# Element-wise work of a fused attention, gate and mixer kernel moved from VectorE to GpSimd and ScalarE

## The chip, the cores and the metric

The kernel runs on one core of a Trainium2 chip. The metric is the device time of one execution in microseconds (us), the median of several runs. Five engines work side by side and each takes its instructions in order: TensorE (PE in the rows, PEld for its weight loads), VectorE (DVE), ScalarE (ACT), GpSimd (POOL) and SyncE (SP), which here issues the DMA transfers.

## What is computed

Three blocks follow one another, all in float32. Shapes: 4 batches, 8 heads, 576 tokens, head width 64, model width 512, a causal convolution of 5 taps.

```python
scores = q @ k.T / sqrt(D)                    # keep the 32 largest of each row
attn = softmax(where(scores >= kth, scores, -1e9)); x = attn @ v

gate = sigmoid(sum_k conv_w[k] * x_shifted[k])          # 5 taps
x = (gate * (x @ w_val)) @ w_out

theta = x @ w_theta
y = w_tok_r @ (x * cos(theta)) + w_tok_i @ (x * sin(theta))
u = x + y
out = u + relu(u @ w_ch)
```

## The kernel before

**Attention.** The heads are taken in 16 pairs (units), four to a batch, and each unit in 9 tiles of 128 rows by 576 columns of scores: 144 tiles. One step of the main loop (lines 1269 to 1271) handles one tile. VectorE carries most of a step: `pick` (L524, L528, L530) finds the 24 largest of each row in pieces, `below` and `rest` (L537, L550) the last 8, `select` (L559 to L564) the threshold for three tiles at once, `mask` (L611) applies it. ScalarE empties the scores (L499), counts (L545) and makes the exponentials (L174); TensorE makes scores (L485, L486), transposes (L624, L628) and the product with v (L704). When a unit is closed (`close`), its normalised result goes to a buffer `xT` (L722), of which there are 5, and the convolution's five taps are summed to the gate: tap 0 and those in `CT` by ScalarE (L747, L750), each of the latter added by GpSimd (L751), the rest by VectorE (L759).

**The later blocks.** The work of gate and mixer is written as generators in a list `jobs`: `front(b)` makes the products `pval` (x @ w_val), `px2t` (@ w_out), `pth` (@ w_theta), the sines and `px2`; `back(b)` makes `py` (the token mix), `ph` (@ w_ch) and the transposes `po` for the output. `work` (lines 1151 to 1168) gives TensorE a ration of them in each step. Jobs run strictly in the order of the list, and `back(0)` and `front(1)` do not begin before every weight is converted (`lacking`, lines 1032 and 775). Where a buffer is needed again, `drain` (lines 140 to 149) writes out all that is left of a job at that point of the program: L697 wants `pval` of the batch before to be done before a unit may take one of the 5 `xT`, L730 the angles before a gate buffer is reused. VectorE and ScalarE execute in the order in which the program is written; the orders of TensorE, GpSimd and SyncE come from a scheduler.

**Three passes.** From batch 1 on (and for `ph` of every batch) a product is made of rounded upper and lower parts of both factors, three passes in a faster format. `halve` (line 345) writes the upper part on ScalarE (L348) and the lower part, the difference, on the engine that `engine` (lines 340 to 343) names (L352): VectorE for the last batch and for the kinds in `ONDVE`, GpSimd otherwise. Kind `w` are the weights (w_ch, w_val, w_out, w_theta, four blocks each, once), `U` the mixer's input to w_ch.

**The conversion.** The weights arrive as pairs of 32-bit words of a 64-bit format and are put together by `cvt` (line 254), in 54 pieces. A piece is loaded by SyncE into one of 6 `raw` buffers (L266), ScalarE takes the absolute value into one of 2 `tmp` buffers and scales the low word (L269, L270), VectorE clamps `tmp` from below (L277), shifts it (L278) and joins it with the high word (L273), GpSimd adds the halves (L291). `convert` advances each piece by one stage per step; a stage that finds `tmp` or `raw` taken waits a step. VectorE's three instructions are put between those of `pick` (list `fill`).

Of the kernel before, what the change touches and what calls it, by code (L numbers as in the profile page):

```python
# [17 lines left out]
ALU = mybir.AluOpType  # L18
# [21 lines left out]
TO = 1  # L40
CT = (1,)
FLAG = 3
AHEAD = 3
SPLIT = (0,)
THREE = (1, 2, 3)
ONDVE = ("w", "U")
PATIENT = True
# [13 lines left out]
LEAST = 2.0 ** -15 * 1.125  # L61
# [2 lines left out]
FRAC = 1  # L64
MORE = 3
GRAIN = 500.0
CT = (1,)
ONDVE = ('w', 'U')
POOLS = ('tok', 'c', 's')
PARTS = (1, 1)  # L70
PATIENT = True
# [6 lines left out]
def attention_gate_phase_mixer(ctx, tc, qT, kT, vt, w_val, conv_t, w_out, w_theta, w_tok, w_ch, out):  # L78
    nc = tc.nc
    P = 128  # L80
    B, S, DM = vt.shape
    U = qT.shape[0]
# [85 lines left out]
    jobs, later, mid, extras, chains, flowing, fill, at_end = [], [], [], [], [], [], [], []  # L168
# [85 lines left out]
    def cvt(name, dst, words, factor, c):  # L254


        p0, a, w = dst.shape
        n = a * w
        r, k = c % len(W["raw"]), c % len(W["tmp"])
        while r in taken:  # L260
            yield None
        taken.add(r)
        raw = W["raw"][r][:p0, :n]
        t = W["tmp"][k][:p0, :n]
        lo, hi = raw[:, :, 0], raw[:, :, 1]
        yield lambda: nc.sync.dma_start(raw.rearrange("p (a w) t -> p a w t", a=a), words)  # L266

        def on_act():
            nc.scalar.activation(t, hi.bitcast(F32), AF.Abs)  # L269
            nc.scalar.activation(lo, lo.bitcast(U32), AF.Copy, scale=2.0 ** -29)  # L270

        def joined():
            nc.vector.scalar_tensor_tensor(hi, hi, -0x40000000, t.bitcast(I32), ALU.bitwise_and, ALU.bitwise_or)  # L273
            taken.remove(("tmp", k))

        def on_dve():
            fill.append(lambda: nc.vector.tensor_scalar(t, t, LEAST, None, ALU.max))  # L277
            fill.append(lambda: nc.vector.tensor_scalar(  # L278
                t.bitcast(I32), t.bitcast(I32), 3, 0x3FFFFFF8, ALU.logical_shift_left, ALU.bitwise_and))
            fill.append(joined)  # L280

        for _ in range(WAIT):
            yield None
        while ("tmp", k) in taken:
            yield None
        taken.add(("tmp", k))
        yield on_act
        yield on_dve
        while ("tmp", k) in taken:
            yield None  # L290
        yield lambda: nc.gpsimd.tensor_tensor(dst.bitcast(I32), *(h.rearrange("p (a w) -> p a w", a=a) for h in (hi, lo)),  # L291
                                                ALU.add)
        taken.remove(r)
        if factor is not None:
            yield lambda: nc.scalar.activation(dst, dst, AF.Copy, scale=factor)
        lacking[name] -= 1
# [43 lines left out]
    def engine(key):  # L340
        if key[0] in POOLS:
            return nc.gpsimd
        return nc.vector if key[1] == B - 1 or key[0] in ONDVE else nc.gpsimd

# [300 lines left out]
    def close(part):  # L645
# [101 lines left out]
        nc.scalar.activation(g, taps[0], AF.Copy, scale=cw[:, hp, 0:1])  # L747
        for k in CT:
            ct = wk.tile([P, S], F32, tag="ct", name=f"ct_{u}_{x}_{k}")[:, : g.shape[1]]
# [3 lines left out]
            yield  # L753
        if not CT:
            yield
            yield
        rest = [k for k in range(1, KW) if k not in CT]
        for k in rest:
# [467 lines left out]
    def convert(i):  # L1226
        begun[0] += PIECES(i)
        while pieces and begun[0] >= 1.0:
            flowing.append(cvt(*pieces.pop(0)))
            begun[0] -= 1.0  # L1230
        for f in list(flowing):
            stage = next(f, 0)
            if stage == 0:
                flowing.remove(f)
            elif stage:
                stage()
# [88 lines left out]
```

## Time and profile before

| | |
|---|---|
| median of 3 runs | 938.37 us (937.66 to 939.21) |
| the profiled execution, its own time | 936.45 us |
| its span, first to last instruction | 934.7 us |
| busy: PE, PEld, DVE, ACT, POOL | 84%, 63%, 87%, 71%, 26% of the span |
| mean granted TensorE clock | 0.912 |

A share of busy time is a mean over stages; what a change in one stage is worth is read from that stage. The row of digits gives the busy share of an engine in tenths in 40 equal slices of some 23 us. A span is 1.75 us shorter than the time of its execution.

### The profile page before, as it was taken

To read this page: it belongs to the slowest core of one execution; us is meant where nothing else is said; L and a number is where in the kernel's file an instruction comes from. 1 tells how busy PE (TensorE), PEld (TensorE's weight loads), DVE (VectorE), ACT (ScalarE), POOL (GpSimd) and SP (SyncE) were. 2 spreads that over 40 slices of the span, in tenths; PEclk is the share of its full clock that TensorE was granted. 3 is DMA by queue.
4 is the path that set the end of the run, shared out by engine and by line. 5 is a ranking of instruction groups with operands and counts; after the bars stand their busy time and mean duration, and the time that the engine had idled before them with its cause. 6 is when DMAs were issued, how large, how long until landed. Compare 5 with 4: busy or idle time off the path is not lost. (4 is left out here: it accounts for less than half of the span.)

```text
span 934.7 us, 16448 instructions
## 1 busy us (share of the span) xinstructions
PE 789.6 (84%) x4620; PEld 586.6 (63%) x4620; DVE 817.5 (87%) x3136; ACT 666.5 (71%) x1682; POOL 247.1 (26%) x390
## 2 busy tenths in 40 slices
PE   3358676786868969997889798998899989999997
PEld 2134454543545537766768667675779767689897
DVE  5699999899999989999999998999999989644522
ACT  3577777678877787777878779667788898534711
POOL 3333233222231211121334332020336301101620
PEclk9987787795878979997979999998989999999999
DMA  7665664443433202422464454222355420006001
GB/s 194 185 162 153 163 165 117 120 124 79 130 86 108 53 15 88 130 74 56 158 177 133 137 166 130 72 45 75 101 153 154 120 91 1 14 23 209 1 1 52
DMA packets 74696, 98.47 MB, mean 105 GB/s; under 512 B 14304, under 2 KB 35168, under 8 KB 74592
## 3 DMA queue, kind: packets, MB, share of 16 engines
q1 hardware_dynamic: 74592, 97.31, 37.5%
q8 instruction: 37, 0.61, 0.3%
q14 instruction: 67, 0.55, 0.2%
HBM read 50.55 MB, written 13.11 MB: 68 GB/s over the span
## 5 line engine op out<-in xcount | busy, mean ns | idle before, releaser
L524 DVE MAX8 cand<-s 128x8 f32<-128x96 f32 x864 | 213.2, 247 | 18.2 <-ACT s L499 11.3
L174 ACT ACTIVATE e<-s,nmax 128x576 f32<-128x576 f32 x144 | 111.5, 774 | 83.1 <-DVE s L611 82.6
L704 PE MATMUL px<-pT,v 128*64 128x256 f32 (+3 forms) x640 | 120.7, 458 | 15.1 <-ACT pT L643 13.9
L624 PE MATMUL pt<-ident,s 128*128 128x128 f32 x576 | 103.2, 306 | 35.2 <-DVE s L611 24.9
L537 DVE SCALAR_TENSOR_TENSOR y<-s,tops 128x576 f32<-128x576 f32 x144 | 127.5, 885 | 0.0
L545 ACT ACTIVATE spent<-s,tops 128x576 bf16<-128x576 f32 x144 | 111.7, 775 | 17.6 <-DVE tops L528 15.9
L611 DVE SCALAR_TENSOR_TENSOR s<-s,thr,e 128x576 f32<-128x576 f32 x144 | 120.9, 840 | 0.0
L499 ACT ACTIVATE s<-ps 128x256 f32<-128x256 f32 (+1 forms) x288 | 102.4, 405 | 24.9 <-PE ps L571 10.2
L1045 PE MATMUL py<-w_tok,z 128*128 128x256 f32 (+1 forms) x432 | 116.7, 409 | 0.9 <-DVE z L904 0.7
L485 PE MATMUL ps<-kh_None,q 128*128 128x256 f32 x240 | 97.0, 412 | 22.9 <-ACT s L499 14.6
L624 PEld LDWEIGHTS pt<-ident,s 128*128 128x128 f32 x576 | 73.2, 155 | 63.6 <-issue 23.0
L550 DVE MAX8 tops<-y 128x8 f32<-128x576 f32 x144 | 108.6, 754 | 0.2
L704 PEld LDWEIGHTS px<-pT,v 128*64 128x64 f32 (+1 forms) x640 | 48.0, 148 | 66.6 <-issue 28.0
L1045 PEld LDWEIGHTS py<-w_tok,z 128*128 128x128 f32 x432 | 77.1, 190 | 18.7 <-DVE z L904 1.1
L528 DVE MAX8 tops<-cand 128x8 f32<-128x48 f32 x432 | 82.5, 191 | 0.2
L643 ACT COPY pT<-pt 128x512 f32<-128x512 f32 x128 | 72.8, 569 | 11.7 <-PE px L704 9.1
L485 PEld LDWEIGHTS ps<-kh_None,q 128*128 128x128 f32 x240 | 49.2, 205 | 48.7 <-ACT s L499 23.5
L486 PE MATMUL ps<-kl_None,q 128*128 128x256 f32 x240 | 74.8, 314 | 0.0
L485 PE MATMUL ps<-kh,q 128*128 128x256 f32 (+1 forms) x72 | 35.0, 489 | 40.5 <-ACT s L499 28.0
L558 POOL TENSOR_SCALAR nmax<-tops 128x3 f32<-128x3 f32 x48 | 12.7, 264 | 190.7 <-DVE tops L528 185.1
L530 DVE MATCH_REPLACE8 cand<-tops,cand 128x48 f32<-128x48 f32 x288 | 55.0, 191 | 0.0
L485 PEld LDWEIGHTS ps<-kh,q 128*128 128x128 f32 x72 | 18.6, 258 | 53.3 <-ACT s L499 34.2
(206 smaller groups left out, 1826.1 us busy)
## 6 DMA issues: line engine op xcount, KB each, us to landing
kh_None<-kh_None SPq DMA_DIRECT2D x48, 144.0 KB, 2.6
kl_None<-kl_None SPq DMA_DIRECT2D x48, 144.0 KB, 2.7
v<-in_vt_dram SPq DMA_DIRECT2D x20, 256.0 KB, 2.8
out_dram<-x2T SPq DMA_DIRECT2D x16, 256.0 KB, 2.9
w<-ch SPq DMA_DIRECT2D x16, 256.0 KB, 4.1
w<-theta SPq DMA_DIRECT2D x16, 256.0 KB, 5.3
kh<-kh SPq DMA_DIRECT2D x28, 144.0 KB, 2.6
kl<-kl SPq DMA_DIRECT2D x28, 144.0 KB, 2.7
```

The lines of the kernel that those rows point to most:

```text
L174: ins = nc.scalar.activation(out, src, func, **more).ins
L485: nc.tensor.matmul(bank[:, :w], q2, kh[:, lo:hi], start=(j == js[0]), stop=False)
L499: nc.scalar.activation(st[:, lo:hi], bank[:, : hi - lo], AF.Copy, scale=0.125)
L524: nc.vector.max(d["cand"][:, k, 8 * x : 8 * x + 8], s_tiles[i][:, x * SUB : (x + 1) * SUB])
L528: nc.vector.max(top, c)
L537: nc.vector.scalar_tensor_tensor(y, s_tiles[i], guess, s_tiles[i], ALU.is_lt, ALU.mult)
L545: nc.scalar.activation(spent, s_tiles[i], AF.Sign, bias=d["tops"][:, k, KC - 1 : KC], scale=-(1.0 + 2.0 ** -22), accum_out=d["acc"][:, k : ...
L550: nc.vector.max(d["tops"][:, k, KC:K], d.pop(("y", k)))
L611: nc.vector.scalar_tensor_tensor(p, p, d["thr"][:, k : k + 1], e.exp, ALU.is_ge, ALU.mult, accum_out=part["sums"][:, e.slot : e.slot + 1])
L624: nc.tensor.transpose(e.pt[:, c, :], p[:, c * P : (c + 1) * P], ident)
L704: nc.tensor.matmul(px[64 * j : 64 * j + 64, :], v[r, c, 64 * j : 64 * j + 64], pT[r, k, :], start=(c == 0), stop=(c == NF), skip_group_che ...
L1045: nc.tensor.matmul(ps, z[:, m * P : (m + 1) * P], W["tok"][:, w, lo:hi], start=(i + k == 0), stop=(i == NF))
```

## The change

The clamp of the conversion goes from VectorE to GpSimd and becomes a stage of its own; no kind of lower part but those of the last batch is left on VectorE; the convolution's third tap (k = 2) is made by ScalarE and added by GpSimd, as the second was.

```diff
-CT = (1,)
-ONDVE = ('w', 'U')
+CT = (1, 2)
+ONDVE = ()
...
         def on_dve():
-            fill.append(lambda: nc.vector.tensor_scalar(t, t, LEAST, None, ALU.max))
             fill.append(lambda: nc.vector.tensor_scalar(
                 t.bitcast(I32), t.bitcast(I32), 3, 0x3FFFFFF8, ALU.logical_shift_left, ALU.bitwise_and))
             fill.append(joined)
...
         yield on_act
+        yield lambda: nc.gpsimd.tensor_scalar(t, t, 3.4e38, LEAST, ALU.min, ALU.max)
         yield on_dve
```

Three places of the instruction order show what this does to the program. The first is ScalarE's queue at tiles 8 to 12 (`tmp0`, `tmp1` are the two `tmp` buffers, `s_9` the scores of tile 9). Before, one piece of the conversion stands in every step:

```order
L499 ACTIVATE s_9_526<-ps_9_256_483 128x320
L269 ACTIVATE tmp0_119<-raw_hi0_113 128x256
L499 ACTIVATE s_10_581<-ps_10_256_533 128x320
L269 ACTIVATE tmp1_120<-raw_hi1_114 128x256
L499 ACTIVATE s_11_660<-ps_11_256_591 128x320
L269 ACTIVATE tmp0_119<-raw_hi2_115 128x256
L499 ACTIVATE s_12_727<-ps_12_256_668 128x320
```

With the change, the same stretch:

```order
L499 ACTIVATE s_9_516<-ps_9_256_478 128x320
L269 ACTIVATE tmp0_119<-raw_lo2_117 128x256
L499 ACTIVATE s_10_569<-ps_10_256_523 128x320
L269 ACTIVATE tmp1_120<-raw_lo3_118 128x256
L499 ACTIVATE s_11_648<-ps_11_256_579 128x320
L499 ACTIVATE s_12_710<-ps_12_256_656 128x320
L269 ACTIVATE tmp0_119<-raw_hi0_113 128x256
```

A `tmp` is held for one step longer, so two pieces pass in three steps. VectorE's last L273 stands at tile 57 before and at tile 84 now, and its first sum of `py` of batch 0 (L1024) at tile 62 before and at 86 now.

The second place is VectorE's queue where `ph` of batch 0 is added (L1076). Before, these sums stand two by two among the attention's instructions:

```order
L550 MAX tops_25_5458<-y_76_5610 128x8
L1076 SCALAR_TENSOR_TENSOR x2T_0_2255<-ph_0_0_0_5556,x2T_0_2255 128x256
L1076 SCALAR_TENSOR_TENSOR x2T_0_2255<-ph_0_1_0_5577,x2T_0_2255 128x256
...
L524 MAX cand_26_5706<-s_78_5552 128x8
...
L550 MAX tops_25_5458<-y_77_5730 128x8
L1076 SCALAR_TENSOR_TENSOR x2T_0_2255<-ph_0_2_0_5628,x2T_0_2255 128x256
L1076 SCALAR_TENSOR_TENSOR x2T_0_2255<-ph_0_3_0_5648,x2T_0_2255 128x256
L524 MAX cand_26_5706<-s_79_5619 128x8
```

With the change they stand at tile 95, at the drain of L697, in a block of 18 without one instruction of the attention (3 of `py`, 8 of `ph`, 7 of `pval` of batch 1):

```order
L550 MAX tops_31_6553<-y_94_6694 128x8
L1024 TENSOR_TENSOR x2T_0_2194<-py_0_1_1_6592,x2T_0_2194 128x320
...
L1024 TENSOR_TENSOR x2T_0_2194<-py_0_3_1_6726,x2T_0_2194 128x320
L1076 SCALAR_TENSOR_TENSOR x2T_0_2194<-ph_0_0_0_6747,x2T_0_2194 128x256
...
L1076 SCALAR_TENSOR_TENSOR x2T_0_2194<-ph_0_3_1_6871,x2T_0_2194 128x320
L788 SCALAR_TENSOR_TENSOR gp_4_3994<-gp_4_3994,pval_1_0_0_6932 128x256
...
L788 SCALAR_TENSOR_TENSOR gp_6_5255<-gp_6_5255,pval_1_2_1_7035 128x320
L584 TENSOR_LOAD flag_30_6707
...
L524 MAX cand_32_7121<-s_96_6655 128x8
```

The work is the same; what moved is the attention, which now stands behind all of it. A second, shorter block of nine (5 of L866 and 4 of L904) stands at tile 101, the drain of L730; before, 3 and 4 stood there.

The third place is GpSimd's queue at the first block: the lower parts that were VectorE's stand in it one behind the other, ahead of the next `nmax` (L558), for which the exponentials wait.

```order
L352 TENSOR_TENSOR U_0_0_6737<-x2T_0_2194,U_0_0_6737 128x512 x2
L352 TENSOR_TENSOR U_0_1_6738<-x2T_0_2194,U_0_1_6738 128x2x320 x2
L352 TENSOR_TENSOR lo0_0_6825<-w_val_122,hi0_0_6824 128x512
L352 TENSOR_TENSOR X_1_0_6827<-xT_4_3603,X_1_0_6827 128x256
...
L352 TENSOR_TENSOR G_1_0_6996<-gp_7_5852,G_1_0_6996 128x256
L352 TENSOR_TENSOR lo0_1_7023<-w_out_123,hi0_1_7022 128x512
...
L352 TENSOR_TENSOR lo2_1_7055<-w_out_123,hi2_1_7054 128x512
L558 TENSOR_SCALAR nmax_31_6555<-tops_31_6553 128x3
```

From tile 103 on, and after the last tile, TensorE's queue holds the same products as before.

## Rows read from the trace of the kernel before

**Rows 1.** The page: busy us, share, instructions; VectorE's busy tenths in 40 slices

```profile
PE 789.6 (84%) x4620; PEld 586.6 (63%) x4620; DVE 817.5 (87%) x3136; ACT 666.5 (71%) x1682; POOL 247.1 (26%) x390
...
DVE  5699999899999989999999998999999989644522
```

**Rows 2.** Stretches: us, then PE, PEld, DVE, ACT, POOL busy, PE clock, DMA

```profile
320.00:360.00 40.00, 30.27 (x162) 18.60 (x160) 36.77 (x146) 30.28 (x68) 6.21 (x12) 0.83 0.25 60
...
800.00:840.00 40.00, 40.00 (x256) 30.72 (x255) 19.80 (x45) 19.03 (x46) 4.25 (x6) 1.00 0.04 10
```

**Rows 3.** The chain that ended last: start us, us, what, in how many instructions

```profile
772.18 0.72 DVE y L537
...
808.57 3.23 PE py L1045 x12
...
840.72 1.46 PE po L1097 x12
842.18 12.80 PE pval L456 x96
...
867.71 5.61 PE pth L456 x24
```

**Rows 4.** Groups of VectorE: times | busy us, mean ns | idle before

```profile
L759 DVE SCALAR_TENSOR_TENSOR gp<-xT,w_conv,gp 128x576 f32<-128x576 f32 (+2 forms) x60 | 43.5, 725 | 3.6 <-DVEq L587 2.3 <-POOL gp L751 0.7
...
L277 DVE TENSOR_SCALAR tmp<-tmp 128x256 f32<-128x256 f32 (+2 forms) x54 | 18.5, 342 | 14.5 <-ACT tmp L269 5.2 <-ACT spent L545 4.5 <-DVEq L587 2.7
...
L352 DVE TENSOR_TENSOR U<-x2T,U 128x512 fp32r<-128x512 f32 (+1 forms) x16 | 12.0, 800 | 0.8 <-ACT U L348 0.7
L352 DVE TENSOR_TENSOR lo<-w_out,hi 128x512 fp32r<-128x512 f32 x4 | 3.9, 988 | 0.0
...
L352 DVE TENSOR_TENSOR lo<-w_val,hi 128x512 fp32r<-128x512 f32 x4 | 2.9, 713 | 0.0
```

**Rows 5.** VectorE in order of time: start us, us, instruction, tiles

```profile
215.82 0.82 DVE L537 SCALAR_TENSOR_TENSOR y<-s,tops 128x576 f32<-128x576 f32 x1
...
220.38 0.17 DVE L563 TENSOR_TENSOR eq<-eq,tops 128x27 f32<-128x27 f32 x1
...
221.00 1.81 DVE L537 SCALAR_TENSOR_TENSOR y<-s,tops 128x576 f32<-128x576 f32 x1
222.73 1.95 DVE L611 SCALAR_TENSOR_TENSOR s<-s,thr,e 128x576 f32<-128x576 f32 x1
```

**Rows 6.** GpSimd in the same stretch, in order of time

```profile
220.77 1.43 POOL L217 TENSOR_TENSOR kl_None<-kl_None,kh_None 128x576 fp32r<-128x576 f32 x1 [0.70 <-ACT kh_None L212]
222.16 1.91 POOL L217 TENSOR_TENSOR ql_None<-ql_None,qh_None 128x576 fp32r<-128x576 f32 x1
```

**Rows 7.** Groups of VectorE with two inputs in on-chip memory, by form

```profile
L537 DVE SCALAR_TENSOR_TENSOR y<-s,tops 128x576 f32<-128x576 f32 x144 | 127.5, 885 | 0.0
...
L561 DVE TENSOR_TENSOR eq<-counts,acc 128x27 f32<-128x27 f32 x48 | 18.8, 391 | 0.0
...
L563 DVE TENSOR_TENSOR eq<-eq,tops 128x27 f32<-128x27 f32 x48 | 15.9, 332 | 0.0
```

**Rows 8.** Groups of GpSimd by form

```profile
L751 POOL TENSOR_TENSOR gp<-gp,ct 128x576 f32<-128x576 f32 x12 | 17.0, 1415 | 36.1 <-ACT ct L750 35.7 <-PE ps L486 0.3
...
L558 POOL TENSOR_SCALAR nmax<-tops 128x3 f32<-128x3 f32 x48 | 12.7, 264 | 190.7 <-DVE tops L528 185.1 <-DMA raw_hi<-in_w_tok_dram 3.5 <-PE px L704 1.3
...
L291 POOL TENSOR_TENSOR w_tok<-raw_hi 128x256 int32<-128x256 int32 x14 | 8.5, 610 | 23.1 <-DVE raw_hi L273 22.3 <-issue 0.7
...
L352 POOL TENSOR_TENSOR L<-x2T,L 128x640 fp32r<-128x640 f32 x4 | 6.2, 1561 | 2.3 <-issue 1.8 <-ACT L L348 0.6
...
L352 POOL TENSOR_TENSOR zl<-cos,zh 128x512 fp32r<-128x512 f32 x4 | 5.2, 1290 | 2.7 <-ACT zh L348 2.7
```

**Rows 9.** VectorE in order of time, where it waits for other engines' products

```profile
568.90 1.88 DVE L866 SCALAR_TENSOR_TENSOR gp<-gp,pth 128x512 f32<-128x512 f32 x3 [2.47 <-ACT gp L859]
...
849.73 0.49 DVE L788 SCALAR_TENSOR_TENSOR gp<-gp,pval 128x320 f32<-128x320 f32 x1 [1.34 <-PE pval L456]
```

## The prediction

> **What bounds the kernel now.** I read the page's busy shares and slices first, then the chain that ended last, then VectorE and GpSimd by line, and last single stretches in order of time. VectorE is busy 87% of the span, but its slices stand at 9 nearly throughout the first 34 and at 4 to 6 after that, with TensorE busy all 40 us of 800 to 840 and VectorE half of them [rows 1, 2]. The chain that ended last passes from VectorE to TensorE at about 774 us and then stays on TensorE but for the sines of the last batch [rows 3]. So there are two stages: up to about 774 us each microsecond taken from VectorE shortens the kernel and each microsecond in which VectorE stands still lengthens it; after that TensorE's products set the end, and they are the same in number with the change. GpSimd is busy 26%, which looks like room [rows 1].
>
> **What VectorE is relieved of.** Its instructions overlap a little: the slow L537 that starts at 221.00 ends at 222.81, while L611 starts at 222.73 [rows 5]. So I count a removed one with its mean less 0.08 us. Clamps: 54 x (0.342 - 0.08) = 14.1 us. Third taps: 20 of the 60 at L759 go, 20 x (0.725 - 0.08) = 12.9. Lower parts of U: 12 of 16 go, 12 x (0.800 - 0.08) = 8.6. Lower parts of weights: 16, four as the 0.988 of w_out and, I take it, twelve as the 0.713 of w_val, 4 x 0.91 + 12 x 0.63 = 11.2 [rows 4]. Sum 46.8 us. The four U of batch 2 and the taps of the last two units lie after 774 us, where VectorE is not the bound: less 4 x 0.72 + 2 x 0.65 = 4.2. There remain 42.6 us.
>
> **What GpSimd's new work takes back.** GpSimd gets 54 clamps; the trace has no clamp of 256 columns on GpSimd, so its price lies between 0.26 us (a scalar operation of 3 columns, L558) and 0.61 (an addition of 256 columns with two inputs, L291); I take 0.45, it being one input, and get 24 us. Then 12 taps of 1.42 and 8 shorter ones of about 0.9, 24 us; 12 lower parts of U at 1.56, 19 us; 16 of weights at 1.29, 21 us [rows 8]. Together 88 us, so GpSimd would be busy some 36%: it does not become the bound by itself. But it slows VectorE. L537 takes 0.82 us alone, and 1.81 beside GpSimd's L217; the L611 behind it takes 1.95 beside the second L217 [rows 5, 6]. By the 0.82 both should take, a pair of 3.3 us on GpSimd has cost VectorE 2.1 us, 0.63 per us. The mean over the run is lower: L537 lies 0.065 above its bare 0.82 in 144 instances, and L561 and L563 lie 0.22 and 0.16 above the bare 0.17 in 48 each, 9.4 + 10.6 + 7.8 = 28 us [rows 5, 7], on 247 us of GpSimd [rows 1], 0.11 per us; that leaves out smaller victims and counts GpSimd's many tiny instructions, which block nothing. Between 0.11 and 0.63 I take 0.25, nearer to the mean than to the worst pair. Of the 88 us some 23 run where VectorE waits anyway (U of batch 0 and six weight blocks in the block below; U of batch 2 and two taps after 774 us). 65 x 0.25 = 16 us. ScalarE's 20 further copies at L750 and the later position of the weight loads in SyncE's queue (the same 54, two in three steps in place of three) I cost at nothing: ScalarE is 71% busy [rows 1], and no load is needed sooner. GpSimd's `nmax` for the exponentials comes behind at most one more instruction in a normal step; a step lasts over 5 us (144 tiles to 774 us). If that cover went, the exponentials would be late next, and with them VectorE's mask. So the relief is 42.6 - 16 = 26 us.
>
> The Trainium skill (SBUF — State Buffer, Who interferes with whom) speaks against this change: a VectorE instruction with two inputs in SBUF and a GpSimd instruction that reads SBUF exclude each other for the whole instruction, whichever started second waiting. The rows agree in kind: 1.81 in place of 0.82. By the rule's worst case, every us of GpSimd blocked, the sum would take back 65 us instead of 16; the rows show that VectorE often has one-input work at that moment.
>
> **What the order costs.** The extra stage makes the conversion end at tile 84 in place of 57, `back(0)` begins 24 tiles later, and the drain of L697 then writes 18 of VectorE's instructions in one block, behind which the whole attention queues. VectorE can do none of them before TensorE has made the products. TensorE's time in the block: of the last group of `py`, nine products in 18 records, 4.8 us at 0.27 each, I take 2 us as still to come; `ph` of batch 0 has as many products of the same shapes as the `pval` of the chain, 12.8 us; the 20 transposes `po` 2.4 us by 1.46 for 12; `pval` of batch 1 up to its seventh group, 7/8 of 12.8, 11.2 us [rows 3]. Before `ph` can go through its first group, two lower parts of U must come from GpSimd, 1.56 each [rows 8], behind a sum and a copy: 3.4 us. Before `pval` go one lower part of a weight at 1.29 and a shorter one of x: 2 us. Sum 34 us, in which VectorE's own 18 instructions (0.49 the longest, less 0.08) fill 7 [rows 9]. So 27 us of standing still, where before there was none there: the same sums stood two by two among the attention, with the products long made. This is what the tail shows: VectorE waits 1.34 us for each group of `pval` when it has nothing else [rows 9]. The clock of TensorE could make it longer: lightly loaded, it was granted 0.83 on the mean of a stretch, between its two levels of 1.2 and 2.4 GHz [rows 2]; I leave that for the range.
>
> The second block, at tile 101, held 3 + 4 instructions before and cost 2.5 us of waiting [rows 9]. Now all five `pth` groups stand in it: 60 products at 5.61 us for 24 make 14 us [rows 3], and the lower parts of w_theta and of its input come from GpSimd ahead of them; VectorE still gets two tiles of attention done while TensorE comes to them. I take 8 us more than before. The bounds for both blocks: 26 us if TensorE is well ahead when VectorE arrives, 54 if it comes at the lower clock and GpSimd's queue delays both. I take 27 + 8 = 35.
>
> **Sum.** 35 - 26 = 9 us longer, or nearly 10 unrounded: 936.45 (the profiled execution's own time) + 9.7 = 946.2. The median of the runs shown is 1.9 above that execution, so I say 948.
>
> **Rivals.**
> (1) The relief wins. If GpSimd disturbs at 0.11 per us, the relief is 42.6 - 7 = 35 us, and with blocks of 26 the run is 9 us shorter: 929. For it: VectorE is full for 770 us, and its waits before were few. Against it: the 34 us of products in front of the first block, which no relief shortens. It decides where both blocks together cost less than the relief of 26 to 35 us. Chance 0.22.
> (2) The sharing is dear. If GpSimd's new instructions meet VectorE's two-input ones as the pair at 221 us did, 0.63 x 65 = 41 us, the relief shrinks to 2 and the run is 33 us longer: 971. For it: the taps, like L217, are long, and ScalarE releases both. Against it: the mean of 0.11 and more. Chance 0.12. The rule cited above would bring about the same, only dearer.
> (3) Relief and blocks cancel to within 0.2%, 938. Chance 0.08.
> That the change does not do what it says is excluded by the order: VectorE's queue has 96 rows fewer, GpSimd's 96 more.
>
> **How the numbers follow.** About 0.2% (1.9 us) is what a measurement of this kernel can tell from no change. The forecast (blocks dearer than the relief, 941 to 960) has a chance of 0.58. Slower by over 0.2%: 0.58 + 0.12 = 0.70; within 0.2%: 0.08; faster: 0.22. The unknown costs alone span from 930 (0.11 per us, blocks 26) to some 990 (0.63, blocks 54); both at their worst is unlikely, so the range is 930 to 966. Within it the likeliest case alone has 941 to 960.
>
> **What would show it.** VectorE's busy sum should fall by about 30 us; L537, L561, L563 and L611 should rise in the mean. In VectorE's order of time there should be a stretch, about 35 us long near the middle of the run, in which 18 short instructions wait for `py`, `ph` and `pval`, with 25 us or more of idle time, and a second of some 10 us soon after. The waits of VectorE on TensorE at L1076, now nearly all in the tail, should grow by some 10 us. TensorE's clock and its time from the last tile to the end (about 160 us) should stay. Wrong would be: no such stretch, or one under 15 us; a last tile that is done no later than before; GpSimd's clamp at over 1 us, which would make the conversion itself late.

## The result, and the profile after

| | before | after |
|---|---|---|
| median | 938.01 us (937.06 to 939.21, 4 runs) | 947.68 us (947.24 to 947.87, 4 runs) |
| the profiled execution, its own time | 936.45 us | 947.87 us |
| its span | 934.7 us | 946.1 us |
| mean granted TensorE clock | 0.912 | 0.902 |

The change is slower: the ratio is 1.010, 95% interval 1.0088 to 1.0112. The prediction was 948.0 us. The traced execution of the kernel before was 1.6 us faster than its median, so the two traces differ by 11.4 us and the medians by 9.7.

Read from the page of the kernel after (busy us, share, instructions; VectorE's busy tenths in 40 slices):

```profile
PE 801.8 (85%) x4620; PEld 591.2 (62%) x4620; DVE 786.6 (83%) x3034; ACT 679.7 (72%) x1702; POOL 329.7 (35%) x492
...
DVE  5699997999899989999995485999999989625522
```

VectorE has 102 instructions fewer and is busy 30.9 us less; GpSimd has 102 more (not 96, as the prediction says) and is busy 82.6 us more [rows 1]. Where the digits stood at 9 there are now 5, 4, 8 and 5 in the middle. The stretches of the kernel after show the same in us (columns as in [rows 2]):

```profile
320.00:360.00 40.00, 27.50 (x135) 17.30 (x133) 37.24 (x141) 33.15 (x78) 9.21 (x19) 0.63 0.37 93
480.00:520.00 40.00, 39.08 (x230) 31.51 (x230) 30.23 (x111) 23.72 (x58) 17.82 (x19) 1.00 0.33 90
520.00:560.00 40.00, 38.97 (x300) 33.87 (x299) 27.36 (x100) 29.16 (x75) 25.72 (x34) 1.00 0.63 208
560.00:600.00 40.00, 38.56 (x213) 31.48 (x211) 26.93 (x89) 32.68 (x66) 16.16 (x15) 1.00 0.53 155
```

Between 480 and 600 us TensorE is busy nearly throughout at its full clock while VectorE lacks 10 to 13 us in each 40. In VectorE's order of time (start, us, instruction; in brackets the idle time before it and what ended that) the hole has this shape:

```profile
506.36 0.87 DVE L1024 TENSOR_TENSOR x2T<-py,x2T 128x320 f32<-128x320 f32 x2
507.90 0.49 DVE L1024 TENSOR_TENSOR x2T<-py,x2T 128x320 f32<-128x320 f32 x1 [0.67 <-PE py L1045]
509.73 0.42 DVE L1076 SCALAR_TENSOR_TENSOR x2T<-ph,x2T 128x256 f32<-128x256 f32 x1 [1.34 <-PE ph L456]
...
520.19 0.49 DVE L1076 SCALAR_TENSOR_TENSOR x2T<-ph,x2T 128x320 f32<-128x320 f32 x1 [2.20 <-PE ph L456]
...
526.06 0.42 DVE L788 SCALAR_TENSOR_TENSOR gp<-gp,pval 128x256 f32<-128x256 f32 x1 [3.69 <-PE pval L456]
...
535.66 0.49 DVE L788 SCALAR_TENSOR_TENSOR gp<-gp,pval 128x320 f32<-128x320 f32 x1 [1.27 <-PE pval L456]
...
569.79 0.69 DVE L866 SCALAR_TENSOR_TENSOR gp<-gp,pth 128x512 f32<-128x512 f32 x1 [4.71 <-POOL L L352]
572.54 0.69 DVE L866 SCALAR_TENSOR_TENSOR gp<-gp,pth 128x512 f32<-128x512 f32 x1 [2.05 <-ACT gp L859]
578.27 1.29 DVE L866 SCALAR_TENSOR_TENSOR gp<-gp,pth 128x512 f32<-128x512 f32 x2 [5.04 <-ACT gp L859]
580.68 0.69 DVE L866 SCALAR_TENSOR_TENSOR gp<-gp,pth 128x512 f32<-128x512 f32 x1 [1.13 <-ACT gp L859]
```

From 506 to 537 us stand 18 short instructions, 16 of them behind a wait for a product; with 0.5 us behind the last of them the waits sum to 22.1 us. The second block waits 12.9 us, against 2.5 before [rows 9]. Summed by line, VectorE's idle time ahead of L1076 grew from 19.4 to 31.2 us and ahead of L788 from 6.4 to 16.3. GpSimd is in the way at the start of the first block and made the four large lower parts of U in one go (GpSimd in order of time):

```profile
506.18 5.63 POOL L352 TENSOR_TENSOR U<-x2T,U 128x512 fp32r<-128x512 f32 x4
```

The chain that ended last has its last long VectorE instruction 11.1 us later than before [rows 3]:

```profile
783.30 0.72 DVE y L537
```

From there to the end of the span are 162.8 us, before 162.5. So all but 0.3 us of the difference lies ahead of it, and it can be booked on VectorE as idle plus busy time. VectorE's waits of over 0.4 us ahead of that point sum to 32.5 us before and 70.6 after: 38.1 more, of which the first block is 22.1, the second 10.5, and 5.5 lie elsewhere (the largest, 3.1 us, stands at 259 us ahead of the conversion's L277). Against them stands less work: of the 30.9 us of busy time some 4 lie behind that point, so 38.1 - 26.7 = 11.4 us, where that `y` comes 11.1 us later and the span is 11.4 us longer.

Of what is left on VectorE, the groups by form (times | busy us, mean ns | idle before) answer to [rows 7]. The first row is the mask in the kernel before, the others are the kernel after:

```profile
L611 DVE SCALAR_TENSOR_TENSOR s<-s,thr,e 128x576 f32<-128x576 f32 x144 | 120.9, 840 | 0.0
```

```profile
L611 DVE SCALAR_TENSOR_TENSOR s<-s,thr,e 128x576 f32<-128x576 f32 x144 | 130.3, 905 | 2.1 <-DVEq L587 2.1
L537 DVE SCALAR_TENSOR_TENSOR y<-s,tops 128x576 f32<-128x576 f32 x144 | 128.3, 891 | 0.0
L561 DVE TENSOR_TENSOR eq<-counts,acc 128x27 f32<-128x27 f32 x48 | 21.7, 453 | 0.3 <-ACT spent L545 0.3
...
L563 DVE TENSOR_TENSOR eq<-eq,tops 128x27 f32<-128x27 f32 x48 | 13.7, 285 | 0.0
```

The mask L611 pays most, 905 ns for 840 before; L561 rose from 391 to 453, L537 hardly (885), and L563 fell from 332. The 6 ns of L537 are no cost: in this one trace the records read some 6 ns longer throughout (L550, with one input, 761 for 754), while the instructions follow each other at the old pace (109 ns at the median from an L530 to the next, in both). On GpSimd (same columns) the clamp took 0.50 us; the tap's mean was 1.42 before [rows 8]:

```profile
L751 POOL TENSOR_TENSOR gp<-gp,ct 128x576 f32<-128x576 f32 x24 | 36.1, 1504 | 24.7 <-ACT ct L750 24.6
L287 POOL TENSOR_SCALAR tmp<-tmp 128x256 f32<-128x256 f32 x52 | 26.0, 500 | 16.7 <-ACT tmp L269 14.7 <-PE ps L486 0.2
```

### The profile page after: what moved, and what is told of

Same layout as the page of the kernel before. It is cut to its first block, busy times and chain, and to the rows that moved or that the text cites. A ratio compares the mean times of both kernels' runs of the same rounds, so it can differ in the third digit from the quotient of the medians.

```text
span 946.1 us, 16477 instructions
## 1 busy us (share of the span) xinstructions
PE 801.8 (85%) x4620; PEld 591.2 (62%) x4620; DVE 786.6 (83%) x3034; ACT 679.7 (72%) x1702; POOL 329.7 (35%) x492
## 5 line engine op out<-in xcount | busy, mean ns | idle before, releaser
L524 DVE MAX8 cand<-s 128x8 f32<-128x96 f32 x864 | 217.8, 253 | 20.7 <-ACT s L499 17.2
L624 PE MATMUL pt<-ident,s 128*128 128x128 f32 x576 | 105.7, 311 | 38.0 <-DVE s L611 26.0
L611 DVE SCALAR_TENSOR_TENSOR s<-s,thr,e 128x576 f32<-128x576 f32 x144 | 130.3, 905 | 2.1 <-DVEq L587 2.1
L537 DVE SCALAR_TENSOR_TENSOR y<-s,tops 128x576 f32<-128x576 f32 x144 | 128.3, 891 | 0.0
L485 PE MATMUL ps<-kh_None,q 128*128 128x256 f32 x240 | 102.6, 434 | 28.7 <-ACT s L499 16.5
L545 ACT ACTIVATE spent<-s,tops 128x576 bf16<-128x576 f32 x144 | 111.9, 777 | 11.2 <-DVE tops L528 9.9
L550 DVE MAX8 tops<-y 128x8 f32<-128x576 f32 x144 | 109.6, 761 | 0.2
L485 PEld LDWEIGHTS ps<-kh_None,q 128*128 128x128 f32 x240 | 51.1, 213 | 61.4 <-ACT s L499 30.9
L528 DVE MAX8 tops<-cand 128x8 f32<-128x48 f32 x432 | 85.0, 197 | 0.6 <-DVEq L587 0.5
L486 PE MATMUL ps<-kl_None,q 128*128 128x256 f32 x240 | 77.4, 324 | 0.0
L751 POOL TENSOR_TENSOR gp<-gp,ct 128x576 f32<-128x576 f32 (+2 forms) x40 | 49.8, 1245 | 47.1 <-ACT ct L750 46.7
L558 POOL TENSOR_SCALAR nmax<-tops 128x3 f32<-128x3 f32 x48 | 14.2, 297 | 146.9 <-DVE tops L528 144.8
L530 DVE MATCH_REPLACE8 cand<-tops,cand 128x48 f32<-128x48 f32 x288 | 56.8, 197 | 0.0
```

The costliest lines, as they stand in the source:

```text
L485: nc.tensor.matmul(bank[:, :w], q2, kh[:, lo:hi], start=(j == js[0]), stop=False)
L524: nc.vector.max(d["cand"][:, k, 8 * x : 8 * x + 8], s_tiles[i][:, x * SUB : (x + 1) * SUB])
L528: nc.vector.max(top, c)
L537: nc.vector.scalar_tensor_tensor(y, s_tiles[i], guess, s_tiles[i], ALU.is_lt, ALU.mult)
L545: nc.scalar.activation(spent, s_tiles[i], AF.Sign, bias=d["tops"][:, k, KC - 1 : KC], scale=-(1.0 + 2.0 ** -22), accum_out=d["acc"][:, k : ...
L550: nc.vector.max(d["tops"][:, k, KC:K], d.pop(("y", k)))
```

## The experiments

All twelve runs go by the same ledger: VectorE's busy time from the page, and its idle time, which is the sum of its waits of over 0.4 us up to the last `y` of the chain. From that `y` to the end of the span are 161.9 to 163.2 us in each of them but run 6 (taken up at the end of this section), so the two columns explain the time. "Before" in the same batches had medians of 937.6 to 938.7 us; the ratio is to those, and a difference between runs of two batches carries up to 1 us of this spread. Busy and idle are from one traced execution each. The numbers in front are those of the runs in the text.

| kernel | us | ratio, 95% interval | DVE busy | DVE idle | POOL busy |
|---|---|---|---|---|---|
| before | 938.0 | | 817.5 | 32.5 | 247.1 |
| after | 947.7 | 1.0088 to 1.0112 | 786.6 | 70.6 | 329.7 |
| 1. after, four `tmp` | 923.9 | 0.9824 to 0.9867 | 796.5 | 36.5 | 339.5 |
| 2. before, with an empty step | 963.5 | 1.0253 to 1.0287 | 815.9 | 59.9 | 246.2 |
| 3. after, clamp back on VectorE | 934.0 | 0.9943 to 0.9979 | 808.9 | 33.4 | 308.8 |
| 4. clamp alone, four `tmp` | 930.1 | 0.9899 to 0.9932 | 806.0 | 35.6 | 273.3 |
| 5. third tap alone | 937.2 | 0.9981 to 0.9999 | 815.0 | 32.9 | 267.9 |
| 6. lower parts alone | 935.6 | 0.9964 to 0.9983 | 810.5 | 32.5 | 285.3 |
| 7. clamp alone, four `tmp`, clamp twice | 932.7 | 0.9924 to 0.9955 | 809.8 | 36.3 | 296.5 |
| 8. clamp alone, four `tmp`, addition twice | 936.1 | 0.9964 to 0.9983 | 814.6 | 35.6 | 311.1 |
| 9. clamp alone, two `tmp` | 952.1 | 1.0125 to 1.0158 | 806.5 | 60.5 | 270.6 |
| 10. after, four `tmp`, moved work cut | 914.8 | 0.9728 to 0.9762 | 782.9 | 39.2 | 364.2 |
| 11. the same, L217 cut too | 908.2 | 0.9656 to 0.9688 | 771.9 | 44.0 | 375.4 |
| 12. before, the same cuts | 928.5 | 0.9862 to 0.9909 | 802.7 | 40.4 | 275.3 |

**1. The blocks taken away.** The relief stays; four `tmp` let the conversion pass one piece in each step again, and it ends at tile 58.

```diff
-        W["tmp"] = [ml.tile([P, half], F32, tag=f"lo{x}", name=f"tmp{x}") for x in range(2)]
+        pair = [ml.tile([P, 2 * half], F32, tag=f"lo{x}", name=f"tmp{x}") for x in range(2)]
+        W["tmp"] = [pair[x % 2][:, x // 2 * half : x // 2 * half + half] for x in range(4)]
```

> The changed kernel with four tmp buffers (two halves of each of the two old ones have become four of their own), so that the conversion again passes one piece in each step and ends at tile 58; back(0) then begins as before, the block of 18 at tile 95 is gone and the second block is back to its old size. Forecast theory (the blocks cost about 35 us, the relief is real and hidden behind them): 947.7 - 22 (idle of the first block) - 10 (growth of the second) = 915, between 910 and 921 us, faster than both kernels; VectorE is busy about as long as in the changed kernel (787 us) and has no stretch of waits over 10 us before 770 us. Rival (sharing between GpSimd and VectorE eats the relief, and the block's waits would be found elsewhere): 935 us or more, with VectorE's means at its two-input lines well above those of the changed kernel.

Measured: 923.9 us, 3 above the upper end. The blocks are gone: idle time fell by 34.0 us, to near the 32.5 of before. But VectorE's busy time rose by 9.9, to 796.5, which the forecast had not in it: 34.0 - 9.9 = 24.1, and the medians differ by 23.8. So the blocks cost about what the prediction said in waiting, and at the same time they covered GpSimd work that otherwise disturbs VectorE. Where the busy time rose can be read from the two traces by VectorE's excess: the time of each two-input instruction over the 20th percentile of its own form, put down to the GpSimd instruction that it overlaps most. It grows by 11.9 us in all: by 4.9 beside the lower parts of weights, 1.1 beside those of U and 2.2 beside those of x, which stood in the block, and by 3.0 beside taps, which did not. The rival (935 or more) falls.

**2. The blocks alone.** No work is moved; a piece only stays a step longer.

```diff
         yield on_act
+        yield None
         yield on_dve
```

> The kernel before with one empty step between ScalarE's and VectorE's stage of the conversion; no work is moved to another engine. The conversion ends at tile 84 and the drain writes the same two blocks as the change does. Forecast theory (the blocks alone cost 35 us on TensorE's products): 938 + 30 to 37 = 968 to 975 us, VectorE busy as before (817 us), a stretch of over 20 us idle at the block of 18. Rival (the blocks cost little by themselves, and the change lost its time to the sharing of GpSimd and VectorE): 938 to 945 us.

Measured: 963.5 us, 25.9 over before; busy time as before (-1.6), idle time 27.4 more. The rival falls: the extra step by itself costs more than the whole change. The forecast was too high, since the blocks wait less here. VectorE's waits from 522 to 600 us in this run (us in total, times, longest; line numbers one higher than in the kernel before):

```profile
DVE gp L867 <- ACT gp L860: 11.3, 4, 5.0
DVE x2T L1077 <- PE ph L457: 7.8, 7, 1.5
DVE gp L789 <- PE pval L457: 6.9, 6, 1.3
```

and from 500 to 590 us in the kernel after:

```profile
DVE gp L788 <- PE pval L456: 10.6, 7, 3.7
DVE x2T L1076 <- PE ph L456: 10.3, 8, 2.2
DVE gp L866 <- ACT gp L859: 8.2, 3, 5.0
DVE gp L866 <- POOL L L352: 4.7, 1, 4.7
```

The first block waits 14.7 us here and 22.1 with the change. The difference of 7 us is not the order's: with the change the lower parts that open `ph` and `pval` come from GpSimd. Here VectorE makes them itself, at a mean of 0.73 us in place of 1.3 to 1.4, and in time in which it would otherwise stand still (VectorE in order of time):

```profile
522.52 2.76 DVE L353 TENSOR_TENSOR U<-x2T,U 128x512 fp32r<-128x512 f32 x4
...
537.15 2.42 DVE L353 TENSOR_TENSOR lo<-w_val,hi 128x512 fp32r<-128x512 f32 x3
```

With one more of `w_val` between them these are 5.9 us, and the block takes 28.4 us from its first instruction to the end of the last, against 29.8 with the change: 5.9 + 1.4 = 7.3. Run 9, which moves the clamp but not the lower parts, waits the same 14.7 us. The wait at 259 us is here as well, 2.9 us at 266, so it too belongs to the extra step.

**3 and 4. Relief without blocks, in two parts.** In the one run the clamp goes back to VectorE and its stage disappears, in the other the clamp alone is moved, with four `tmp` as above.

```diff
         def on_dve():
+            fill.append(lambda: nc.vector.tensor_scalar(t, t, LEAST, None, ALU.max))
...
-        yield lambda: nc.gpsimd.tensor_scalar(t, t, 3.4e38, LEAST, ALU.min, ALU.max)
```

> The changed kernel with the clamp back on VectorE and its extra stage gone: the third tap and the lower parts stay on GpSimd, the conversion ends at tile 57, no block of 18. Forecast theory: the relief is 12.9 + 8.6 + 11.2 - 4.2 = 28.5 us, of which sharing at 0.11 to 0.25 VectorE-us per GpSimd-us takes 5 to 14 on some 55 us: 938 - 24 to 938 - 14 = 914 to 924 us. Rival (dear sharing, 0.63): 938 - 28.5 + 35, 938 us or slower.

> The kernel before with only the clamp moved to GpSimd and four tmp buffers, so that no block arises. Forecast theory: 14.1 us of VectorE relieved, 54 clamps of 0.50 us on GpSimd take back 3 to 7: 938 - 11 to 938 - 7 = 927 to 931 us. Rival (a clamp on GpSimd disturbs VectorE as much as it relieves it): 936 to 942 us.

Measured: 934.0 and 930.1 us. The clamp brings 7.5 us, as forecast: by the prediction's prices 14.1 us were removed, busy time fell by 11.5, so 2.6 came back for 26.2 us of GpSimd, 0.10 per us. Taps and lower parts bring 3.6 in place of 14 to 24: 32.7 us removed before the share in the tail, busy time down by 8.6 only, so 24.1 came back for 61.7 us of GpSimd, 0.39 per us. The forecast fell here, and this run lies nearer to its rival.

**5 and 6. Which of the two.** `CT = (1, 2)` alone, and `ONDVE = ()` alone, in the kernel before.

> The kernel before with only the third tap moved to ScalarE and GpSimd. In the run with the clamp back on VectorE, taps and lower parts together relieved VectorE of 28.5 us and brought only 3.6; this run and the next tell which of the two gives the relief back. Theory now (a two-input GpSimd instruction costs VectorE 0.38 us per us, whichever line it is): 11.6 us relieved, 24 us on GpSimd take back 9: 937.6 - 2.5 = 935 us. Rival 1 (the taps are the dear ones, they run beside the mask): 938 us or slower. Rival 2 (the taps cost as the prediction had it, 0.25): 937.6 - 5.6 = 932 us.

> The kernel before with only the lower parts of weights and U on GpSimd. Theory now (0.38 us per us of GpSimd): 16.9 us relieved, 39 us on GpSimd of which 6 lie after VectorE's stage take back 13: 937.6 - 4 = 934 us. Rival 1 (the lower parts are the dear ones): 938 us or slower. Rival 2 (they cost 0.25): 937.6 - 8.6 = 929 us.

Measured: 937.2 and 935.6 us, 0.9 and 2.5 us faster, together the 3.4 that run 3 had as 3.6. The tap lies nearer to its rival 1 (938 or slower) than to its theory (935), the lower parts nearer to theirs (934). Both give most of it back: the tap 12.9 - 2.5 = 10.4 us for 20.8 us of GpSimd, the lower parts 19.8 - 7.0 = 12.8 for 38.2. The taps are somewhat dearer (0.50 against 0.34 per us); rival 2 of both falls.

**7 and 8. GpSimd work that relieves nothing.** In the kernel of run 4 GpSimd makes one instruction of the conversion twice, with the same result: the clamp (one input), or the addition L291 (two inputs).

```diff
-        yield lambda: nc.gpsimd.tensor_scalar(t, t, 3.4e38, LEAST, ALU.min, ALU.max)
+        def on_pool():
+            nc.gpsimd.tensor_scalar(t, t, 3.4e38, LEAST, ALU.min, ALU.max)
+            nc.gpsimd.tensor_scalar(t, t, 3.4e38, LEAST, ALU.min, ALU.max)
+
+        yield on_pool
```

> The run with the clamp alone and four tmp buffers (930.1 us), in which GpSimd makes each clamp twice, with the same result: 27 us of GpSimd work with one input are added and VectorE is relieved of nothing. Theory now (one-input work on GpSimd costs VectorE 0.10 us per us): 930.1 + 2.7 = 933 us. Rival (every GpSimd instruction costs 0.38 per us): 940 us.

> The run with the clamp alone and four tmp buffers (930.1 us), in which GpSimd makes the conversion's addition of two halves twice, with the same result: 54 instructions of 0.61 us with two inputs, 33 us of GpSimd, are added and VectorE is relieved of nothing. Theory now (two-input work costs 0.38 per us): 930.1 + 12.5 = 943 us. Rival (0.10 per us, as the clamps; the dear ones are dear by their place or length and not by their two inputs): 933 us.

Measured: 932.7 (+2.5) and 936.1 (+5.9). The clamps behave as expected. The additions lie between theory and rival: VectorE's busy time rose 3.8 us for 23.2 us of GpSimd (0.16 per us) in the first, 8.6 for 37.8 (0.23) in the second. So the additions are the dearer ones per us; they have two inputs, but they are also a little longer (0.61 us against 0.50) and stand elsewhere in the step, and no run separates these. A short addition costs some two thirds of what the long ones of 1.3 to 1.8 us do. That pointed to length.

**9. Additivity.** Run 4 with the two old `tmp`.

> The kernel before with only the clamp moved, in its own stage and with the two old tmp buffers: both blocks arise, taps and lower parts stay on VectorE. Theory now (the delay costs 25.9 us, as in the run with the empty step; the clamp brings back 7.5, as with four tmp buffers): 938 + 25.9 - 7.5 = 956 us, so the taps and lower parts together would be worth 956 - 947.7 = 8 us where the blocks stand, against 3.6 where they don't, since part of their disturbance falls into VectorE's waits. Rival (what GpSimd does costs the same with and without the blocks): 938 + 25.9 - 7.5 = 956 less nothing, and the change itself would be at 952, not 947.7; or the clamp's relief vanishes in the blocks: 960 us or more.

Measured: 952.1 us. The theory's 956 is missed by 4, and the rival I had written down was not worked out well enough to be tested by it. Against run 2 the clamp brings 11.4 us here, not 7.5; the taps and lower parts bring 952.1 - 947.7 = 4.4, not the 8 expected, and no more than without blocks: 3.6 in run 3, and 930.1 - 923.9 = 6.2 between runs 4 and 1. The ledger says why: with the blocks busy time falls by 19.9 us for them, not by 9.5 (806.5 to 786.6, against 806.0 to 796.5 with four `tmp`), but idle time grows by 10.1. Work that is taken from VectorE inside a block turns into waiting: the first block waits 14.7 us in this run and 22.1 in the kernel after.

**10 and 11. Length.** From run 1, GpSimd's tap additions and lower parts in halves, then also L217. The excess in the forecast is the one explained at run 1. Worked out from the trace of run 1 it is somewhat lower than stated there: 0.54 us per tap of 576 columns, and 21.5 us beside L217. The diff shows the taps; the lower parts are cut likewise.

```diff
-            nc.gpsimd.tensor_tensor(g, g, ct, ALU.add)
+            half = g.shape[1] // 2
+            for s in (slice(0, half), slice(half, g.shape[1])):
+                nc.gpsimd.tensor_tensor(g[:, s], g[:, s], ct[:, s], ALU.add)
```

> The changed kernel with four tmp buffers (923.9 us), in which each tap addition and each lower part that GpSimd makes is cut into two instructions of half the columns. Theory (VectorE's two-input instruction waits for the rest of one GpSimd instruction, so shorter ones cost less: in that run the excess of VectorE over its own undisturbed time is 0.65 us per tap of 576 columns, 0.44 per lower part of 512, 0.68 of 640, and 0.17 to 0.25 per piece of 256 or 320): 20 taps and 32 lower parts save about 10 us, 914 us, between 911 and 919. Rival (the cost goes by GpSimd's busy time, which the cutting lengthens by some 0.19 us per cut): 924 to 930 us.

> As the run before, with the 38 subtractions of keys and queries (L217 in the kernel before, 1.6 us each, with 24.5 us of VectorE's excess beside them) cut in two as well. Theory of length: another 10 us less, 904 us, between 900 and 912. Rival (cost by busy time): 928 to 936 us.

Measured: 914.8 and 908.2 us, inside the theory's bounds; the rival falls. GpSimd is busy 24.7 and then 11.2 us more, and yet VectorE's busy time falls by 13.6 and then 11.0. The excess falls where the cuts are: beside taps from 15.9 to 10.0 us in run 10, beside L217 from 20.9 to 12.7 in run 11. One meeting of the same two L217 with `y` and the mask shows it. Run 1, VectorE and then GpSimd, in order of time:

```profile
215.86 1.78 DVE L538 SCALAR_TENSOR_TENSOR y<-s,tops 128x576 f32<-128x576 f32 x1
217.56 1.95 DVE L612 SCALAR_TENSOR_TENSOR s<-s,thr,e 128x576 f32<-128x576 f32 x1
```

```profile
215.60 1.41 POOL L217 TENSOR_TENSOR kl_None<-kl_None,kh_None 128x576 fp32r<-128x576 f32 x1 [0.58 <-ACT kh_None L212]
216.98 1.91 POOL L217 TENSOR_TENSOR ql_None<-ql_None,qh_None 128x576 fp32r<-128x576 f32 x1
```

And run 11, the same two, with four instructions of 288 columns on GpSimd:

```profile
212.79 1.17 DVE L541 SCALAR_TENSOR_TENSOR y<-s,tops 128x576 f32<-128x576 f32 x1
213.88 1.34 DVE L615 SCALAR_TENSOR_TENSOR s<-s,thr,e 128x576 f32<-128x576 f32 x1
```

```profile
212.54 2.06 POOL L218 TENSOR_TENSOR kl_None<-kl_None,kh_None 128x288 fp32r<-128x288 f32 x2 [0.59 <-ACT kh_None L212]
214.57 2.06 POOL L218 TENSOR_TENSOR ql_None<-ql_None,qh_None 128x288 fp32r<-128x288 f32 x2
```

Alone each of VectorE's two takes some 0.81 us. Uncut they pay 1.78 + 1.95 - 1.62 = 2.1 us, cut 0.9: VectorE gets in between the halves. Taken one by one, the four halves last 0.80, 1.30, 1.31 and 0.80 us, so GpSimd pays too where it meets VectorE. The Trainium skill (SBUF — State Buffer, Who interferes with whom) has it that the engine that issues first holds the shared port pair for its whole instruction, and the other waits. A shorter instruction would then hold it for less, and the rows agree: 0.9 us in place of 2.1.

**12. The cuts without the change.**

> The kernel before, nothing moved, with the same cuts as the last run: GpSimd's tap additions, lower parts and subtractions of keys and queries made in two instructions of half the columns each. It tells what of the 30 us between the kernel before and the last run is the cutting and what the moved work. Theory of length: the 38 subtractions give back 6.6 us as from the run before the last to the last, the 20 taps and the lower parts that already were GpSimd's some 4: 938.3 - 11 = 927 us, so that the moves with four tmp buffers are worth 927 - 908 = 19 us once cut, against 13.7 uncut. Rival (the cuts help only the moved work): 935 to 938 us.

Measured: 928.5 us, 1.5 above the theory's 927 and far below the rival. So of the 30 us between before and run 11 the cuts alone are 10, and the moves are worth 928.5 - 908.2 = 20 us once cut and without blocks, against 938.0 - 923.9 = 14 uncut. Run 11 is the fastest of all.

In the run with the lower parts alone the chain's last `y` stands at 747.7 us, since the chain crosses to TensorE elsewhere; its idle time is counted to there.

## Why the prediction was right, by its steps

**The two stages.** Right: the tail is 162.8 us, and the loss lies ahead of it.

**The order's cost, 27 + 8 us.** Right in place and mechanism: 22.1 and 10.5, in the 18 and 9 instructions named; run 2 makes the blocks with nothing else and run 1 takes them away. The first was sized 5 too high, and so the sign of 25 us or more of idle time was missed: the block is 30 us long, not 34. TensorE's products came out near their price; its waits for the lower parts from GpSimd, priced at 3.4 and 2 us, were short. From 505 to 537 us (us in total, times, longest):

```profile
PEld pval L456 <- POOL X L352: 1.2, 1, 1.2
PEld ph L456 <- POOL U L352: 0.3, 1, 0.3
```

The second block was sized 2.5 too low. The clock did not add to it: TensorE was granted its full clock in the blocks, and 0.63 on the mean of 320 to 360 us, where it had less to do. Not foreseen were the 5.5 us of small waits outside the blocks; by run 2 the largest belongs to the extra step. Together 38.1 in place of 35.

**What is removed, 46.8 us, and what comes back, 16.** Busy time fell by 30.9, so 15.9 came back. The sum is right and its parts are not. One price of 0.25 for all 65 uncovered us was the mean of unlike things: a clamp costs 0.10, taps and lower parts 0.39 where nothing covers them. The clamps were booked too high and the others too low, and in the kernel with its blocks the two cancel. That L537 and L563 would rise was wrong: it was the mask and L561 that paid. ScalarE's 20 further copies, priced at nothing, cost nothing that shows: with the tap alone VectorE's idle time is 32.9 us, before 32.5.

**What lies under cover.** The prediction let 23 us of GpSimd's new work run free, some 14 of them in the first block and 9 behind 774 us. The first is true while the block stands: in the trace 14.6 us of new lower parts lie in it. When it is removed, that work comes out: VectorE's busy time rises 9.9 us, and of the 11.9 us by which the excess grows some 8 are beside lower parts that the block had covered. That is why run 1 missed its forecast, and why both effects (24 us of blocks, 14 us of relief, by the medians) are smaller alone than the 38 and 27 that the trace books for them together.

**The rivals.** "The relief wins" falls: without blocks the relief is 14 us, with them 26.7, in neither case as much as the blocks' waiting. "The sharing is dear" falls as priced (0.63), but its kind is real for the long instructions: at 0.34 to 0.50 it eats most of what taps and lower parts relieve.

**The number.** That 948.0 meets 947.7 is in part luck. The prediction's own terms give 35 - 26.35 = 8.7 us; its "nearly 10 unrounded" does not come out of them. In the traces the two terms are 38.1 and 26.7: a first block with 5 us less waiting than priced stands against a second with 2.5 us more and 5.5 us of waits that were not foreseen. What the runs confirm is the place, the mechanism and the sign.

## What to carry to other kernels

Before a stage is added to a pipeline whose buffers are held from stage to stage, count how many pieces then pass in each step and what begins when the last one is through; here one more buffer pair (in the same two tiles of memory, cut otherwise) turned +10 us into -14. Work moved to an engine that shares something with the bound engine has to be priced per kind and length of instruction, not per microsecond, and long instructions are worth cutting even though the cut costs the moving engine time. A change of two parts can cover one with the other, so take each alone before believing a sum.

## What the runs showed of the hardware that was not expected

In this kernel GpSimd's long additions and subtractions (most of 512 to 640 columns) cost VectorE 0.34 to 0.50 us of busy time per us of GpSimd (0.34 the lower parts, 0.50 the taps), the conversion's additions of 256 columns 0.23, its clamps with one input 0.10 to 0.16. Where work was removed, these rest on the prediction's prices for it. Cutting 576 columns into 288 raised GpSimd's time (taps: 1.525 us once in run 1, 0.936 us twice in run 10) and still lowered the whole time, by 9.1 us for the moved work and 6.6 for L217:

```profile
L752 POOL TENSOR_TENSOR gp<-gp,ct 128x576 f32<-128x576 f32 x24 | 36.6, 1525 | 29.5 <-ACT ct L751 29.3
```

```profile
L756 POOL TENSOR_TENSOR gp<-gp,ct 128x288 f32<-128x288 f32 x48 | 43.9, 936 | 28.9 <-ACT ct L753 28.7
```

The first row is run 1, the second run 10. Smaller cuts than halves were not tried, so where the gain ends stays open.
